# Kernel generation of a state-space mixer on one core: the lower half of the phase table stored with its four channels backwards, and its samples written out in two parts

## The chip, the cores and the metric

The program runs on one core of one Trainium2 chip. The metric is the device time of one execution in microseconds (us); lower is better. The engines are named as the profile names them: PE (matrix products; PEld is its weight load), DVE (elementwise work), ACT (activation functions and copies), POOL, and SP, which here only issues DMAs. "The profile" is one execution recorded by the hardware; its times count from the first instruction of the program.

## What is computed

One block of a sequence model: a state-space mixer and a channel MLP, each with a residual, on 2048 positions of 512 channels. Cut to what matters:

```python
dt = exp(log_dt)[:, None]                     # one step size per channel d
logdA = dt * (A_re + 1j * A_im)               # 512 channels x 128 states
P = exp(logdA[:, :, None] * l)                # powers at the positions l
K = einsum("dn,dnl,dn->dl", C, P, dt * B).real   # the convolution kernel, one per channel
y = irfft(rfft(u padded) * rfft(K padded))    # causal convolution along the positions
h = x + y + u * Dskip                         # u: layernorm of layernorm-ed x
out = h + gelu(layernorm(layernorm(h)) @ w1 + b1) @ w2 + b2
```

The change touches the second and third line from the top: how samples of K are made.

## The kernel before

The channels are done in two halves of 256 (`hh` = 0 and 1). A half is 64 groups `e` of four channels `g`. The kernel K is not made at all 2048 positions but at sample positions, as a product of two exponentials: a coarse one in 32 steps `k` of 8 positions, and a fine one at 20 offsets `m`.

- **`exps` (lines 659 to 688).** ACT fills the magnitudes: `K.Pt[128 states, 2, 64 e, 32 k, 4 g]`, its second plane `[:, 1]`, by 32 exponentials a half (line 673, one for each `k`, 256 columns, the four channels side by side), and `K.Q[128, 2, 64 e, 20 m, 4 g]` by 20 more (line 681). DVE multiplies Q by an amplitude (line 685).
- **`p_half` (lines 691 to 719).** A half has 8 blocks `b` of 8 groups `e`. For each, PE writes phases into PSUM (`pv`, line 703), ACT takes cosines and sines of them (line 142, tile `s`, two planes of 512 columns: 8 `e` x 16 `i` x 4 `g`), and DVE multiplies them into the magnitudes (`mul`, lines 709 to 714, all through the helper on line 79). The 16 phases serve 32 exponents: the upper ones, `k` = 16 + `i`, take `s` as it is, in one operation of 1024 columns for both planes; the lower ones, `k` = 15 - `i`, take the two planes of `s` exchanged, and run downwards in `k`. [...]
- **`q_half` (lines 722 to 751).** The same for Q: phases `qv`, sines `sq`, one product of 1024 columns on DVE for each of ten pieces a half.
- **`kgen` (lines 754 to 801).** For each group of four channels PE multiplies the Pt block (128 states x 128 columns `4k + g`) with the Q block (128 states x 80 columns) into `kps`. ACT or DVE moves eight groups at a time to the tile `samples`, called `all` in the code, `[128 rows 4k + g, 4 g, 20, 64 e]`: eight such moves a half. Of the four `g` of a row only that row's own is wanted: `put` (line 784) writes, for each `g`, the rows `g::4` to DRAM (`KD`), four transfers a half. `get` (line 794) then loads five arrangements of it back as `kt`, the operand of the next products.
- **`conv` (lines 895 to 1000).** PE makes the kernel's spectrum from `kt` and a table `M` (`kfps`, line 930), DVE multiplies it with the spectrum `X` of the input (`pa`, `pb`, `X`), PE turns it back (`zps`), ACT copies it (`z`), and it goes through DRAM (`Zd`, line 997) to `ZT` (line 995). The input's spectrum is made in `x_stage` (`xps`, lines 882 to 885) from `X`, which is loaded from `A_dram` in four transfers of 1 MB (line 865).

All instructions of this part are recorded as operations with engines that a list of numbers, `ORDER`, puts into one fixed order; each engine works through its own in that order, and so does the DMA queue of SP. Four things stand near the transfers of the samples. On SP, in the first half: two `put`, two transposing transfers (`R<-M`, line 479), a `get`, the fourth load of X, two small loads of `M` (line 462), a `get`; POOL has the other two `put` and three `get`. In the second half SP has all four `put`, then a `ZT` load, a `get`, two stores of `z`, and four `get`.

The MLP follows (lines 1194 to 1312).

Of the kernel before, what the change touches and what calls it, by code (L numbers as in the profile page):

```python
# [10 lines left out]
ACT = mybir.ActivationFunctionType  # L11
ALU = mybir.AluOpType
# [4 lines left out]
P = 128  # L17
# [60 lines left out]
def tt(nc, out, a, b, op, e="DVE"):  # L78
    (nc.vector if e == "DVE" else nc.gpsimd).tensor_tensor(out, a, b, op)  # L79


def bc(ap, shape):
    return ap.to_broadcast(shape)
# [3 lines left out]
def evac(nc, eng, out, in_):  # L87
    if eng in (0, "ACT"):
        nc.scalar.copy(out, in_)  # L89
    else:  # L90
        nc.vector.tensor_copy(out, in_)  # L91
# [35 lines left out]
def logs(nc):  # L127
    if NOW[0] != "logs":
        nc.scalar.preload_act_table_set("natural_log_exp_and_others")
    NOW[0] = "logs"  # L130
# [8 lines left out]
def sines(nc, out, v):  # L139
    NOW[0] = "sines"  # L140
    n = v.shape[-1]
    nc.scalar.activation(out, v.bitcast(i16)[..., 0:2 * n:2], ACT.Sin, scale=S2PI / 65536)  # L142
# [516 lines left out]
def exps(nc, S, K, big, hh, gate):  # L659
    ds = slice(HW * hh, HW * hh + HW)  # L660

    def get():
        K.Pt = big.tile([P, 2, HW // 4, 32, 4], bf16, name="Pt", tag="b1")
        K.Q = big.tile([P, 2, HW // 4, 20, 4], bf16, name="Q", tag="b2")

    K.o_get = S.op("NONE", 0.0, get, gate)
    K.o_pe, K.o_qe = [], []
    S.group = f"pe{hh}"
    for i in range(16):
        def amp(i=i):  # L670
            logs(nc)
            for k in (15 - i, 16 + i):
                nc.scalar.activation(K.Pt[:, 1, :, k, :], K.th[:, ds].rearrange("p (e g) -> p e g", g=4), ACT.Exp, scale=float(8 * k))  # L673

        K.o_pe.append(S.op("ACT", 0.62, amp, [K.o_th, K.o_get], fun=AT["exp"][hh]))
    S.group = f"qe{hh}"
    for n in range(5):
        def amp(n=n):
            logs(nc)
            for m in range(4 * n, 4 * n + 4):  # L680
                nc.scalar.activation(K.Q[:, 1, :, m, :], K.th[:, ds].rearrange("p (e g) -> p e g", g=4), ACT.Exp, scale=float(OFFS[m]))  # L681

        def mul(n=n):
            e = K.Q[:, 1, :, 4 * n:4 * n + 4, :]
            nc.vector.tensor_tensor(e, e, bc(K.amp[:, ds].rearrange("p (e g) -> p e g", g=4).unsqueeze(2), [P, HW // 4, 4, 4]), ALU.mult)

        x = S.op("ACT", 1.25, amp, [K.o_th, K.o_get], fun=AT["exp"][hh], bias=5.0)
        K.o_qe.append(S.op("DVE", 0.62, mul, [x, K.o_amp]))


def p_half(nc, S, K, sc, psp, hh):

    K.o_p = [[], []]
    for qd in range(2):
        S.group = f"p{hh}{qd}"
        for g in range(4):
            cell = {}
            b = 4 * qd + g

            def ph(cell=cell, b=b):  # L700
                v = cell["v"] = psp.tile([P, 2, 512], f32, name="pv", tag="p", bufs=PB)
                for u in range(2):
                    nc.tensor.matmul(v[:, u], lhsT=K.PQ[hh][:, b, :], rhs=K.RP[:, u].rearrange("p e i g -> p (e i g)"), start=True, stop=True)

            def sn(cell=cell):
                cell["s"] = sc.tile([P, 2, 8, 16, 4], bf16, name="s", tag="w", bufs=WB)
                sines(nc, cell["s"][:].rearrange("p u e i g -> p u (e i g)"), cell["v"][:])

            def mul(cell=cell, b=b):
                s, e = cell["s"], slice(8 * b, 8 * b + 8)  # L710
                hi = K.Pt[:, :, e, 16:32, :].rearrange("p u e k g -> p u e (k g)")
                tt(nc, hi, s[:].rearrange("p u e i g -> p u e (i g)"), bc(hi[:, 1:2], [P, 2, 8, 64]), ALU.mult)
                for u in range(2):
                    tt(nc, K.Pt[:, u, e, 15::-1, :], s[:, 1 - u], K.Pt[:, 1, e, 15::-1, :], ALU.mult)

            p = S.op("PE", 0.9, ph, [K.o_pl[hh], K.o_out[0], K.o_pe[8]], acq="p", bias=-10)
            K.o_phase[hh].append(p)
            x = S.op("ACT", 0.94, sn, [p] + K.o_pe + K.o_six, acq="w", rel=[p], fun=AT["sin"][hh])
            K.o_p[qd].append(S.op("DVE", 1.23, mul, [x] + K.o_pe, rel=[x]))
# [34 lines left out]
def kgen(nc, S, K, cv, sc, psp, hh, KD):  # L754
    cell = {}
    ends, mm = [], []
    for s in range(2):
        for b in range(4):
            e0 = 32 * s + 8 * b

            def mms(s=s, b=b, e0=e0):
                kps = cell[s, b] = psp.tile([P, 8, 128], f32, name="kps", tag="p", bufs=PB)
                for e in range(8):
                    for u in range(2):
                        nc.tensor.matmul(kps[:, e, 0:80], lhsT=K.Pt[:, u, e0 + e].rearrange("p k g -> p (k g)"),
                                         rhs=K.Q[:, u, e0 + e].rearrange("p m g -> p (m g)"), start=(u == 0), stop=(u == 1))

            def out(e, s=s, b=b, e0=e0):
                if not s and not b:
                    cell["all"] = sc.tile([P, 4, 20, 64], bf16, name="samples", tag="ko", bufs=1)  # L770
                evac(nc, e, cell["all"][:, :, :, e0:e0 + 8], cell[s, b][:, :, 0:80].rearrange("p e (m g) -> p g m e", g=4))

            first = not s and not b
            m = S.op("PE", 0.7, mms, [K.o_p[s][b], K.o_q[s][b], K.o_q[s][4]], acq="p")
            mm.append(m)
            ends.append(S.op(("ACT", "DVE"), (0.75, 0.75), out, [m] + (K.o_raw if first else ends[:1]), rel=[m], acq="ko" if first else None))
    K.o_kgen = mm
    ds = slice(HW * hh, HW * hh + HW)

    def q(e):  # L780
        return nc.sync if e == "SP" else nc.gpsimd

    def put(e, g):
        q(e).dma_start(KD[hh][32 * g:32 * g + 32].rearrange("p (r c) -> p r c", r=4)[:, :, 0:320], cell["all"][g::4, g].rearrange("p (r s) j -> p r (s j)", s=5))

    def get(e, t):
        if t == 0:
            K.kt[hh] = cv.tile([P, 5, HW], bf16, name="kt", tag="kt", bufs=2)
        if t < 2:
            src = KD[hh][:].rearrange("(g k) (r c) -> (k r) g c", g=4, r=8)[128 * t:128 * t + 128, :, 0:64]  # L790
        else:
            at = (64, 128, 256)[t - 2]
            src = KD[hh][:].rearrange("(g k) (r c) -> (k r) g c", g=4, r=4)[:, :, at:at + 64]
        q(e).dma_start(K.kt[hh][:, t, :].rearrange("p (g c) -> p g c", g=4), src)

    either = ("SP", "POOL")
    w = [S.op(either, (0.46, 0.8), lambda e, g=g: put(e, g), ends, rel=[ends[0]], lat=2.5) for g in range(4)]
    K.o_put = w
    K.o_kt[hh] = []
    for t in range(5):  # L800
        K.o_kt[hh].append(S.op(either, (0.46, 0.8), lambda e, t=t: get(e, t), w + K.o_kt[hh][:1], lat=2.5, acq="kt" if t == 0 else None))
# [651 lines left out]
```

## Time and profile before

| | |
|---|---|
| runs of the kernel before | 263.83, 269.31 and 265.45 us, median 265.45 |
| the profiled execution | 264.65 us |
| its span, first to last instruction | 262.9 us; 1.75 us lie around it |
| granted TensorE clock, mean | 0.991 |
| busy: PE, DVE, ACT | 222.3, 201.4, 178.5 us |

The sums below are made against the profiled execution, 264.65 us, which lies 0.8 us under the median of the three runs. In the rows of the profile, L79 and L91 are lines of helpers, so work is told apart by the names of its tiles: `Pt<-s,Pt` is the product of this change, `KD<-samples` its transfer. A row of the timeline reads: start, duration of the row, engine, line, operation, tiles, shape, count, and in brackets how long the engine had been idle and what ended that. Rows of equal instructions that follow each other are merged.

### The profile page before, as it was taken

How to read it: one execution, taken by the hardware profiler on the slowest of the kernel's cores; microseconds unless marked ns; L12 is line 12 of the kernel's file. 1: busy time of each engine (PE TensorE's matmuls, PEld its weight loads, DVE VectorE, ACT ScalarE, POOL GpSimd, SP SyncE). 2: the span in 40 equal slices, each digit the busy share in tenths (PEclk: the TensorE clock that was granted, in tenths of full speed). 3: DMA queues.
4: the chain of work that ended last, by engine and by line, in shares of the span. 5: the costliest groups of instructions: out<-in, count | busy, mean ns of one | idle time of the engine just before them, and what ended most of it. 6: DMA issues, size and time to landing. Idle time of an engine off the chain costs nothing.

```text
span 262.9 us, 4459 instructions
## 1 busy us (share of the span) xinstructions
PE 222.3 (85%) x1574; PEld 139.1 (53%) x1587; DVE 201.4 (77%) x445; ACT 178.5 (68%) x303; POOL 35.3 (13%) x96
## 2 busy tenths in 40 slices
PE   3999118856698598689999999879999999999994
PEld 2333002322496386468988888668844444444443
DVE  5999999999999969999789989757745764771022
ACT  4999999999999959998643666546704603622810
POOL 8806920000016000000520000000000000000000
PEclk9999999999999989999999999999999999999999
DMA  5804933588787700061197576979532033023001
GB/s 160 299 1 83 175 108 122 106 259 257 232 285 138 170 0 2 0 172 30 52 209 205 145 218 188 251 218 329 134 80 80 1 60 102 0 45 88 31 22 57
DMA packets 50450, 33.61 MB, mean 128 GB/s; under 512 B 22186, under 2 KB 49068, under 8 KB 50172
## 3 DMA queue, kind: packets, MB, share of 16 engines
q1 hardware_dynamic: 49068, 29.82, 41.8%
q0 software_dynamic: 1360, 3.51, 5.6%
q8 instruction: 12, 0.20, 0.3%
q14 instruction: 10, 0.08, 0.1%
HBM read 18.65 MB, written 11.26 MB: 114 GB/s over the span
## 4 chain that ended last, share of the span: by engine, by line
PE 44%; ACT 25%; DVE 13%; DMA 11%; issue 4%; SPq 2%; ACTq 0%; DVEq 0%
PE h1ps L1260 14%; PE o2ps L1273 13%; PE kfps L930 5%; ACT Pt L673 4%; DMA Zd<-z 4%; ACT a L89 4%; ACT sq L142 3%; DMA X<-A_dram 3%; ACT s L142 3%; ACT Q L681 2%; DVE pa L79 2%; DVE X L79 2%; DVE pb L79 2%; ACT z L89 2%; DVE Pt L79 1%
## 5 line engine op out<-in xcount | busy, mean ns | idle before, releaser
L1263 ACT ACTIVATE hT<-h1ps,b_sb 128x512 bf16<-128x512 f32 (+3 forms) x55 | 31.9, 604 | 41.0 <-PE h1ps L1260 39.2
L1260 PE MATMUL h1ps<-y2T,wide 128*128 128x512 bf16 (+3 forms) x217 | 40.2, 336 | 0.7 <-DVE ve L75 0.6
L930 PE MATMUL kfps<-kt,M 128*128 128x256 bf16 x320 | 38.7, 276 | 0.0
L1273 PE MATMUL o2ps<-w_sb,hT 128*128 128x512 bf16 (+3 forms) x183 | 38.5, 366 | 0.2
L79 DVE TENSOR_TENSOR ot<-o2ps,h 128x512 bf16<-128x512 f32 (+1 forms) x17 | 10.9, 658 | 30.6 <-PE o2ps L1273 21.2
L930 PEld LDWEIGHTS <-M 128*128 128x128 bf16 x320 | 31.8, 99 | 4.5 <-issue 0.2
L1260 PEld LDWEIGHTS <-wide 128*128 128x128 bf16 (+1 forms) x220 | 21.8, 100 | 17.0 <-issue 0.8
L1273 PEld LDWEIGHTS <-hT 128*128 128x128 bf16 (+1 forms) x187 | 18.3, 98 | 19.7
L79 DVE TENSOR_TENSOR Pt<-s,Pt 128x512 bf16<-128x512 bf16 (+1 forms) x48 | 22.8, 510 | 0.7 <-ACT s L142 0.2
L844 PE MATMUL aps<-u,BD 128*128 128x512 bf16 x30 | 10.1, 422 | 14.5 <-DVE u L839 11.0
L673 ACT ACTIVATE Pt<-th 128x256 bf16<-128x256 f32 x64 | 21.1, 405 | 0.9 <-DVE th L79 0.9
L142 ACT ACTIVATE sq<-qv 128x1024 bf16<-128x1024 int16 x20 | 20.9, 1079 | 0.0
L89 ACT CAST z<-zps 128x1024 bf16<-128x1024 f32 (+1 forms) x16 | 15.5, 976 | 2.8 <-PE zps L969 2.4
L142 ACT ACTIVATE s<-pv 128x1024 bf16<-128x1024 int16 x16 | 16.6, 1080 | 0.0
L89 ACT CAST a<-aps 128x1024 bf16<-128x1024 f32 x16 | 15.7, 1040 | 0.1
L738 PE MATMUL qv<-RQ,PQ 128*128 128x512 bf16 (+1 forms) x64 | 11.8, 298 | 4.2 <-ACT s L142 1.8
L844 PEld LDWEIGHTS <-BD 128*128 128x128 bf16 x32 | 2.9, 101 | 21.0 <-DVE u L839 15.4
L91 DVE CAST X<-xps 128x1024 bf16<-128x1024 f32 x11 | 12.9, 1217 | 1.3 <-PE xps L885 1.3
L449 POOL DMA_DIRECT2D Dp<-Dd x24 | 12.2, 517 | 9.8 <-DMA Dd<-ds 9.8
L79 DVE TENSOR_TENSOR Q<-sq,Q 128x1024 bf16<-128x1024 bf16 x20 | 13.1, 685 | 0.2
L681 ACT ACTIVATE Q<-th 128x256 bf16<-128x256 f32 x40 | 13.0, 403 | 0.0
L89 ACT CAST kf<-kfps 128x512 bf16<-128x512 f32 (+1 forms) x9 | 5.7, 633 | 10.7 <-PE kfps L930 7.0
(242 smaller groups left out, 441.0 us busy)
## 6 DMA issues: line engine op xcount, KB each, us to landing
A_dram<-a SPq DMA_DIRECT2D x16, 256.0 KB, 2.6
X<-A_dram SPq DMA_DIRECT2D x4, 1024.0 KB
Zd<-z SPq DMA_DIRECT2D x15, 256.0 KB, 3.8
ZT<-Zd SPq DMA_DIRECT2D x10, 256.0 KB, 4.0
x<-in_A_u_dram SPq DMA_DIRECT2D x4, 512.0 KB
X<-in_A_u_dram SPq DMA_DIRECT2D x4, 512.0 KB
out_dram<-ot SPq DMA_DIRECT2D x15, 128.0 KB, 1.7
ZT<-Zd POOLq DMA_DIRECT2D x6, 256.0 KB, 4.6
```

The lines of the kernel that those rows point to most:

```text
L79: (nc.vector if e == "DVE" else nc.gpsimd).tensor_tensor(out, a, b, op)
L89: nc.scalar.copy(out, in_)
L91: nc.vector.tensor_copy(out, in_)
L142: nc.scalar.activation(out, v.bitcast(i16)[..., 0:2 * n:2], ACT.Sin, scale=S2PI / 65536)
L449: nc.gpsimd.dma_start(t[o::128 // cnt], bass.AP(row.tensor, row.offset + 1024 * kh, [[0, cnt], [1, 1024]]))
L673: nc.scalar.activation(K.Pt[:, 1, :, k, :], K.th[:, ds].rearrange("p (e g) -> p e g", g=4), ACT.Exp, scale=float(8 * k))
L681: nc.scalar.activation(K.Q[:, 1, :, m, :], K.th[:, ds].rearrange("p (e g) -> p e g", g=4), ACT.Exp, scale=float(OFFS[m]))
L844: nc.tensor.matmul(ps[:, h, :], lhsT=K.BD[:, h].rearrange("p a b -> p (a b)"), rhs=cell["u"][:], start=True, stop=True)
L930: nc.tensor.matmul(ps[:, k, c, :], lhsT=K.M[:, t, k0 + k, c, :], rhs=kt[:, t, :], start=((plain or c == 1) and t == 0), stop=(t == 4))
L1260: nc.tensor.matmul(pt[:fs, 0:n], lhsT=K.w1_sb[:, dc, fc * P:fc * P + fs], rhs=(y2T[tb][:, dc, js, :] if tb or js.start else K.y2T[:, dc]). ...
L1263: nc.scalar.activation(hT[tb % 2][:fs, fc, cols], pt[:fs, 0:n], ACT.Gelu_apprx_tanh, bias=K.b1_sb[:fs, fc:fc + 1], scale=1.0)
L1273: nc.tensor.matmul(pt[:], lhsT=h[:fs, fc, jj * P:(jj + 1) * P], rhs=K.w2_sb[:fs, fc, d], start=(fc == 0), stop=(fc == NFC - 1))
```

## The change

The diff:

```diff
@@ exps @@
             for k in (15 - i, 16 + i):
-                nc.scalar.activation(K.Pt[:, 1, :, k, :], K.th[:, ds].rearrange("p (e g) -> p e g", g=4), ACT.Exp, scale=float(8 * k))
+                nc.scalar.activation(K.Pt[:, 1, :, k, :] if k > 15 else K.Pt[:, 1, :, k, ::-1], K.th[:, ds].rearrange("p (e g) -> p e g", g=4), ACT.Exp, scale=float(8 * k))
@@ p_half @@
                 s, e = cell["s"], slice(8 * b, 8 * b + 8)
                 hi = K.Pt[:, :, e, 16:32, :].rearrange("p u e k g -> p u e (k g)")
                 tt(nc, hi, s[:].rearrange("p u e i g -> p u e (i g)"), bc(hi[:, 1:2], [P, 2, 8, 64]), ALU.mult)
-                for u in range(2):
-                    tt(nc, K.Pt[:, u, e, 15::-1, :], s[:, 1 - u], K.Pt[:, 1, e, 15::-1, :], ALU.mult)
+                lo = K.Pt[:, :, e, 0:16, :].rearrange("p u e k g -> p u e (k g)")[:, :, :, ::-1]
+                tt(nc, lo, s[:, ::-1].rearrange("p u e i g -> p u e (i g)"), bc(lo[:, 1:2], [P, 2, 8, 64]), ALU.mult)
@@ kgen @@
     def put(e, g):
-        q(e).dma_start(KD[hh][32 * g:32 * g + 32].rearrange("p (r c) -> p r c", r=4)[:, :, 0:320], cell["all"][g::4, g].rearrange("p (r s) j -> p r (s j)", s=5))
+        for rows, at in ((slice(32 * g, 32 * g + 16), slice(3 - g, 64, 4)), (slice(32 * g + 16, 32 * g + 32), slice(64 + g, P, 4))):
+            q(e).dma_start(KD[hh][rows].rearrange("p (r c) -> p r c", r=4)[:, :, 0:320], cell["all"][at, g].rearrange("p (r s) j -> p r (s j)", s=5))
```

What it does. The magnitudes of the lower exponents, `k` < 16, are stored with their four channels backwards. Then (`k`, `g`) of the lower half, read from its last column to its first, is `i` and `g` of the phases in rising order, and both planes of the lower half are one operation of 1024 columns: its output and its second input step by -1 element in the innermost dimension (64 columns), and the first input takes the planes of `s` in exchanged order. In the samples, the rows of `k` < 16 come out as `4k + 3 - g`, those of `k` >= 16 as `4k + g`; so `put` has two transfers for each `g`, of 16 rows each, where it had one of 32.

The list `ORDER` is the same, so nothing changes its place; operations get shorter or longer lists of instructions. Three places show it.

On DVE, the first three blocks of the first half (`Pt<-s,Pt` is the product with the sines, `u` the normalised input, `PQ` the phases' operand). Before:

```order
L91 COPY PQ_203<-lps 128x2048
L79 TENSOR_TENSOR Pt<-s,Pt 128x2x8x64
L79 TENSOR_TENSOR Pt<-s,Pt 128x8x16x4 x2
L839 TENSOR_SCALAR u<-x,mv,rs_230 128x512
L79 TENSOR_TENSOR Pt<-s,Pt 128x2x8x64
L79 TENSOR_TENSOR Pt<-s,Pt 128x8x16x4 x2
L79 TENSOR_TENSOR Pt<-s,Pt 128x2x8x64
L79 TENSOR_TENSOR Pt<-s,Pt 128x8x16x4 x2
```

And now (a row of x2 is one block, a row of x4 two):

```order
L91 COPY PQ_203<-lps 128x2048
L79 TENSOR_TENSOR Pt<-s,Pt 128x2x8x64 x2
L840 TENSOR_SCALAR u<-x,mv,rs_230 128x512
L79 TENSOR_TENSOR Pt<-s,Pt 128x2x8x64 x4
L840 TENSOR_SCALAR u<-x,mv,rs_230 128x512
```

Three instructions of a block became two of the same shape; there are 16 blocks in the program.

On SP, from the first half's `put` to its last `get` (`KD` is the samples in DRAM, `kt` what is loaded from it, `R` a transposed table, `X` the input). Before:

```order
L865 DMA X<-A_dram 128x8x512 x3
L784 DMA KD_65<-samples 128x1x320 x2
L479 DMA_TRANSPOSE R<-M 128x4x128 x2
L794 DMA kt<-KD_65 128x4x64
L865 DMA X<-A_dram 128x8x512
L462 DMA M<-Bd 1x64x128 x2
```

And now:

```order
L866 DMA X<-A_dram 128x8x512 x3
L785 DMA KD_65<-samples 64x1x320 x4
L479 DMA_TRANSPOSE R<-M 128x4x128 x2
L795 DMA kt<-KD_65 128x4x64
L866 DMA X<-A_dram 128x8x512
L462 DMA M<-Bd 1x64x128 x2
```

Two more transfers stand ahead of the transposing ones, a `get` and the fourth load of X. POOL likewise has four `KD<-samples` where it had two, ahead of its three `get`.

On SP in the second half, where `KD_66` is that half's samples. Before:

```order
L784 DMA KD_66<-samples 128x1x320 x4
L995 DMA ZT<-Zd_67 16x8192
L794 DMA kt<-KD_66 128x4x64
L997 DMA Zd_67<-z 128x4x256 x2
L794 DMA kt<-KD_66 128x4x64 x4
```

And now:

```order
L785 DMA KD_66<-samples 64x1x320 x8
L996 DMA ZT<-Zd_67 16x8192
L795 DMA kt<-KD_66 128x4x64
L998 DMA Zd_67<-z 128x4x256 x2
L795 DMA kt<-KD_66 128x4x64 x4
```

Four more transfers stand ahead of all five `get` of that half.

## The prediction

> **What bounds the kernel now.** First the page: busy shares, the tenths in 40 slices of 6.57 us, and the shares of the chain that ended last.
>
> ```profile
> span 262.9 us, 4459 instructions
> PE 222.3 (85%) x1574; PEld 139.1 (53%) x1587; DVE 201.4 (77%) x445; ACT 178.5 (68%) x303; POOL 35.3 (13%) x96
> DVE  5999999999999969999789989757745764771022
> ACT  4999999999999959998643666546704603622810
> PE 44%; ACT 25%; DVE 13%; DMA 11%; issue 4%; SPq 2%; ACTq 0%; DVEq 0%
> ```
>
> The changed work lies between 49 and 126 us, slices 8 to 20. There DVE and ACT are both full, so a mean share decides nothing. The windows of the two stretches with the products, of the stretch in which ACT sets the pace, and of the one after:
>
> ```profile
> 49.00:77.60 28.60, 20.38 (x203) 11.66 (x206) 27.80 (x59) 28.48 (x34) 0.00 (x0) 1.00 0.85 251
> 97.10:126.00 28.90, 25.44 (x271) 18.87 (x272) 27.90 (x55) 26.69 (x30) 0.00 (x0) 1.00 0.17 46
> 98.40:120.70 22.30, 18.84 (x173) 13.39 (x175) 21.67 (x44) 22.27 (x24) 0.00 (x0) 1.00 0.22 60
> 128.00:145.00 17.00, 16.78 (x154) 14.70 (x152) 14.99 (x27) 7.36 (x10) 3.67 (x4) 1.00 0.76 180
> ```
>
> (Length, then busy PE, PEld, DVE, ACT, POOL.) In the first half DVE idles 0.8 us of 28.6 and ACT 0.1; in the second ACT idles 0.03 us of 22.3 and DVE 0.6; after 128 PE idles 0.2 of 17. So DVE work that grows is paid in full at once, while DVE work that shrinks uncovers ACT after the first fraction of a microsecond.
>
> How the first half ends, on DVE, then on ACT:
>
> ```profile
> 70.91 2.87 DVE L79 TENSOR_TENSOR Pt<-s,Pt 128x1024 bf16<-128x1024 bf16 x6
> 73.70 1.28 DVE L79 TENSOR_TENSOR Q<-sq,Q 128x1024 bf16<-128x1024 bf16 x2
> 74.90 0.69 DVE L73 TENSOR_SCALAR Mn<-M 128x2048 bf16<-128x2048 bf16 x1
> 75.50 1.29 DVE L79 TENSOR_TENSOR M<-base,Dp 128x1024 bf16<-128x1024 bf16 x2
> 76.71 0.82 DVE L91 CAST samples<-kps 128x640 bf16<-128x640 f32 x1
> ```
>
> ```profile
> 70.95 2.07 ACT L142 ACTIVATE sq<-qv 128x1024 bf16<-128x1024 int16 x2
> 72.77 3.81 ACT L89 CAST samples<-kps 128x640 bf16<-128x640 f32 x6
> ```
>
> The samples are complete at 76.71 + 0.82 = 77.53 by DVE, though ACT's part is done at 72.77 + 3.81 = 76.58. What follows on SP's queue, on POOL, and on PE:
>
> ```profile
> 77.60 1.17 SPq L784 DMA_DIRECT2D KD<-samples  x2
> 78.83 2.58 SPq L479 DMA_TRANSPOSE R<-M  x2
> 81.60 0.43 SPq L794 DMA_DIRECT2D kt<-KD  x1
> 82.49 1.17 SPq L865 DMA_DIRECT2D X<-A_dram  x1
> ```
>
> ```profile
> 78.10 1.33 POOL L784 DMA_DIRECT2D KD<-samples  x2 [43.87 <-issue]
> ...
> 81.59 2.27 POOL L794 DMA_DIRECT2D kt<-KD  x3 [2.16 <-DMA KD<-samples]
> ```
>
> ```profile
> 90.83 0.33 PE L882 MATMUL xps<-X,M 128*128 128x256 bf16 x1 [2.44 <-DMA X<-A_dram]
> ```
>
> PE waits 2.44 us for the fourth load of X, which stands on SP behind the samples' transfers. This queue, and not DVE or PE, carries the delay from 77.6 to 90.8.
>
> The second half, on SP, with the landing time of the last `get` and the PE row that needs it:
>
> ```profile
> 127.53 2.64 SPq L784 DMA_DIRECT2D KD<-samples  x4
> 130.28 0.57 SPq L995 DMA_DIRECT2D ZT<-Zd  x1
> 131.66 0.37 SPq L794 DMA_DIRECT2D kt<-KD  x1
> 132.49 0.91 SPq L997 DMA_DIRECT2D Zd<-z  x2
> 133.45 2.60 SPq L794 DMA_DIRECT2D kt<-KD  x4
> ...
> 137.37 2.33 SPq L1015 DMA_DIRECT2D wide<-Ds  x4
> ```
>
> ```profile
> L794 SPq DMA_DIRECT2D kt<-KD x2: 507/542/577, 134.9 to 135.5; - x2
> ...
> DMA to landing us min/median/max: 2.8/2.8/2.8
> ```
>
> ```profile
> 138.75 1.47 PE L930 MATMUL kfps<-kt,M 128*128 128x256 bf16 x12
> ```
>
> The last `get` starts at 135.5 and lands at 138.3; PE begins to use it at 138.75, without a gap. The margin is 0.45 us.
>
> **The change, part by part.** (1) *The product.* A block now: two operations of 512 columns and one of 1024. The row at 70.91 holds two blocks, and the next row starts at 73.70, so a block takes (73.70 - 70.91) / 2 = 1.40 us. An operation of 1024 columns takes (74.90 - 73.70) / 2 = 0.60 us from start to start. If the new one runs like the old upper one, a block takes 1.20 us: 0.20 us less, 1.6 us in each half. Its price is not in the trace: no DVE row here is known to step backwards in its innermost dimension. The nearest rows:
>
> ```profile
> L79 DVE TENSOR_TENSOR Pt<-s,Pt 128x512 bf16<-128x512 bf16 x32 | 13.5, 422 | 0.5
> L79 DVE TENSOR_TENSOR Pt<-s,Pt 128x1024 bf16<-128x1024 bf16 x16 | 11.0, 685 | 0.2 <-ACT s L142 0.2
> L91 DVE CAST X<-xps 128x1024 bf16<-128x1024 f32 x11 | 12.9, 1217 | 1.3 <-PE xps L885 1.3
> ```
>
> Between 512 and 1024 columns of bf16 lie 263 ns, 0.51 ns a column; the operation on f32 out of PSUM pays 1217 ns for 1024, about 1.04 ns a column after the same start. These are the ends, 685 and 1217 ns. I take 685: the row of 422 ns is the nearest, since it already writes and reads with `k` falling, in runs of four columns, at the fast rate (512 columns at the slow rate would be 422 + 0.53 x 512 = 693 ns).
>
> [...]
>
> What 1.6 us less on DVE gives in the first half: its last Q product waits for ACT's last `sq`, 70.95 + 2.07 = 73.02. From there Q 0.60, Mn 0.60 (75.50 - 74.90) and the two M 1.21 (76.71 - 75.50) put the move of samples at 75.43 and its end at 76.25. Then ACT's end at 76.58 is late next: SP starts at 76.66 instead of 77.60, 0.94 us earlier. In the second half I take 0: ACT is full from 98.4 to 120.7, PE from there on, so they cover what DVE saves.
>
> (2) *The exponentials.* Half of the Pt exponentials write each four columns backwards.
>
> ```profile
> L673 ACT ACTIVATE Pt<-th 128x256 bf16<-128x256 f32 x64 | 21.1, 405 | 0.9 <-DVE th L79 0.9
> ...
> L489 ACT ACTIVATE M<-M 128x256 bf16<-128x256 bf16 x2 | 1.3, 794 | 2.2 <-DMA M<-in_A_log_dt_dram 2.2
> ```
>
> I take 0: as before, they write runs of four with a jump between them, and another direction within a run is nearer to that than anything else. The far end is the scattered exponential of line 489, 794 ns: 32 x 0.39 = 12.4 us of ACT, hardly hidden in the first half. A gain would need fewer than 405 ns for 256 columns, for which nothing speaks.
>
> (3) *The transfers, first half.* Each half of a `put` costs SP an issue of its own. Two puts took 78.83 - 77.60 = 1.23 us. That half the rows make an issue cheaper is not what the queue shows: four `wide<-Ds` took 2.33 us, 0.58 each, and these are of 8 KB:
>
> ```profile
> wide<-Ds SPq DMA_DIRECT2D x8, 8.0 KB
> ...
> KD<-samples SPq DMA_DIRECT2D x6, 80.0 KB, 2.0
> ```
>
> So two more cost 1.23 us (ends: 0.0, if two halves issue like one whole, and 1.23). With the 0.94 us from (1), the transposes, the `get` and the load of X come 0.29 us later: X is issued at 82.78. POOL's two more, at 1.33 / 2 = 0.67 each, end at 78.10 - 0.94 + 2.67 = 79.83 and land some 2.1 us later, at 81.9, 0.3 us behind the 81.59 of before; the same shift. PE, waiting for X, passes it on. First half: +0.3 us.
>
> (4) *The transfers, second half.* Four more on SP: 130.28 - 127.53 = 2.75 us. Part falls into waits of SP: between 130.85 and 131.66 it waited for the last put to land, between 132.03 and 132.49 for `z`; 1.27 us, of which some 0.15 us stay as gaps between issues. The first `get` now needs only the first parts: the seventh put starts at 127.53 + 6 x 0.69 = 131.66 and lands, after the 2.0 us of the row above, at 133.7, just when SP comes to it. So the `get` are late by 2.75 - 1.12 = 1.6 us; the last lands at 139.9. PE wants it at 138.75, or 0.4 us later for the fifth product: it waits 0.8 to 1.2 us, I take 1.0. PE has no gap in the 17 us around (window above), and DVE and the stores of `z` wait for its `kfps`, so this goes to the end.
>
> Sum: 264.65 + 0.3 + 1.0 = 265.95, say **266.0 us**. Against the median of the runs, 265.45, it would be 0.5 more.
>
> **The rivals.** *A: the backward operation runs at the slow rate.* The product loses once the new operation takes more than 1.40 - 0.60 = 0.80 us from start to start, and the whole is over 2% slower from about 1.03 on (2% of 264.65 is 5.3 us; less the transfers' 2.2, with DVE's idle 0.6 added, it is 3.7 over 16 blocks, 0.23 on top of 0.80). At 1217 ns it takes from start to start what this row gives, (4.61 - 1.22) / 3 = 1.13 us:
>
> ```profile
> 79.23 4.61 DVE L91 CAST X<-xps 128x1024 bf16<-128x1024 f32 x4
> ```
>
> A block takes 0.60 + 1.13 = 1.73 us, 0.33 more, 2.7 us a half. DVE's idle time takes a little of it, as an estimate 0.4 of the 0.8 us idle in the first window and 0.2 of the 0.6 in the third; 2.3 and 2.5 us remain, and both halves end on DVE. The transfers' 1.23 and 1.0 are paid on top: 264.65 + 2.3 + 1.2 + 2.5 + 1.0 = 271.65, about 271.6 us. For it: no backward row in the trace. Against it: the 422 ns. This one ends slower by over 2%.
>
> *B: two half transfers issue like one.* Then the first half keeps its 0.94 us and the second loses nothing: 263.7 us. For it: the same number of bytes and rows in all. Against it: the 8 KB issues at 0.58 us.
>
> *C: the work on DVE gets shorter, but nothing in front of SP does* (ACT's moves end later than before, since PE makes `kps` in the same places). Then 264.65 + 1.2 + 1.0 = 266.9 us. It lies within the range of the forecast.
>
> **How the numbers follow.** The forecast with C, 264.3 to 267.5 us: 0.62. A, with rates between the two as well, 268 to 272.5: 0.28. B, 263 to 264.3: 0.07. Slow exponentials, or something else: 0.03. The range from 263.6 to 271.8 us leaves out the tails of A and B and the last case, some 2 in 10. The forecast's own range is 264.3 to 267.5. Faster by over 2%, about what a measurement of this kernel can tell from no change, would be under 260: no case gives it, 0.02. Slower by over 2%, over about 270, is most of A: 0.23. Within 2%: 0.75.
>
> **What would show it.** In the profile after: the row `Pt<-s,Pt 128x1024`, x32, at 685 ns on average (A: near 950, half of them at 1217); the first `KD<-samples` on SP near 76.7 (A: near 79.9); its four rows at 2.4 us together (B: 1.2); PE's wait for X still there; a new wait of PE for `kt` of about 1 us at the first `kfps` of the second half; and ACT's `Pt<-th` at 405 ns. I am wrong if the backward step costs a rate, or if SP's issues shrink with their rows.

## The result, and the profile after

The kernel after takes 267.22 us (median of 20 runs, 264.79 to 269.92), the kernel before, beside it on the same chip, 264.33 us (20 runs, 262.30 to 269.31). The ratio is 1.007, 95% interval 1.0043 to 1.0098: some 1.9 us slower, a small difference but a sure one. The ratio is taken over the executions within 1.5% of their kernel's fastest (16 of the 20 after, 17 of the 20 before); the medians are over all, and lie further apart, 2.9 us. The profiled execution of the kernel after took 265.38 us, with a span of 263.6.

First the price that no row had shown, the product that steps backwards, and the exponentials that write backwards. The page's groups, after:

```profile
L673 ACT ACTIVATE Pt<-th 128x256 bf16<-128x256 f32 x64 | 21.1, 405 | 0.9 <-DVE th L79 0.9
L79 DVE TENSOR_TENSOR Pt<-s,Pt 128x1024 bf16<-128x1024 bf16 x32 | 20.3, 688 | 0.4 <-ACT s L142 0.2
```

All 32 products of 1024 columns take 688 ns on average, where the 16 upward ones of before took 685: a step of -1 in the innermost dimension costs nothing that can be seen here. The exponentials stay at 405 ns. The line with the instruction counts has DVE at 429 instructions and 200.1 us busy (445 and 201.4 before).

This execution runs late by 0.9 us before the changed work begins. The copy ahead of the first product, in before and then in after:

```profile
47.88 1.22 DVE L91 COPY PQ<-lps 128x2048 bf16<-128x2048 bf16 x1
```

```profile
48.77 1.22 DVE L91 COPY PQ<-lps 128x2048 bf16<-128x2048 bf16 x1
```

Below, 0.89 us are taken off a time of after where it is compared with before. I read nothing from it: of the nine experiments with the changed product, five profiled executions have this copy at 47.9 us and four at 48.7. (The four profiled executions with the product of before all have it at 47.9, too few to tell whether the change has a part in it.)

The end of the first half, after: DVE, then SP's queue, then POOL.

```profile
70.34 0.69 DVE L79 TENSOR_TENSOR Q<-sq,Q 128x1024 bf16<-128x1024 bf16 x1 [0.25 <-ACT sq L142]
71.25 0.69 DVE L79 TENSOR_TENSOR Q<-sq,Q 128x1024 bf16<-128x1024 bf16 x1 [0.22 <-ACT sq L142]
71.86 2.49 DVE L79 TENSOR_TENSOR Pt<-s,Pt 128x1024 bf16<-128x1024 bf16 x4
...
77.28 0.82 DVE L91 CAST samples<-kps 128x640 bf16<-128x640 f32 x1
```

```profile
78.17 2.50 SPq L785 DMA_DIRECT2D KD<-samples  x4
80.71 3.62 SPq L479 DMA_TRANSPOSE R<-M  x2
84.95 0.37 SPq L795 DMA_DIRECT2D kt<-KD  x1
85.38 0.49 SPq L866 DMA_DIRECT2D X<-A_dram  x1
```

```profile
78.67 2.37 POOL L785 DMA_DIRECT2D KD<-samples  x4 [43.53 <-issue]
82.83 2.27 POOL L795 DMA_DIRECT2D kt<-KD  x3 [1.79 <-DMA KD<-samples]
```

SP begins its four transfers at 78.17, less 0.89 is 77.28: 0.32 us earlier than the 77.60 of before, not 0.94. DVE now catches up with ACT's `sq` twice before its last blocks, and waits; from the start of that copy to the end of the last move of samples it is busy 27.85 us instead of 28.85, but idle 1.48 instead of 0.80. The four transfers take 2.50 us, as forecast; but the transposing ones behind them take 3.62 where they took 2.58, so the fourth load of X goes out at 85.38 - 0.89 = 84.49, 2.0 us later than the 82.49 of before.

The chain that ended last, from 78 to 95 us, runs through just this queue. Before, then after (start, duration, what):

```profile
78.83 1.27 SPq L479
...
80.14 1.26 SPq L479
...
82.49 8.30 DMA X<-A_dram
```

```profile
80.71 1.28 SPq L479
...
82.03 2.30 SPq L479
...
85.38 6.72 DMA X<-A_dram
```

Of the two transposing transfers only the second grew, from 1.26 to 2.30 us. In this execution the load itself took 6.72 us instead of 8.30, which gives back a good part of the delay; PE resumes here, waiting longer than before (2.44):

```profile
92.14 0.40 PE L883 MATMUL xps<-X,M 128*128 128x256 bf16 x1 [3.11 <-DMA X<-A_dram]
```

The second half, after: SP's queue, then PE at the first product that needs the last `get`.

```profile
128.60 5.48 SPq L785 DMA_DIRECT2D KD<-samples  x8
134.18 0.54 SPq L996 DMA_DIRECT2D ZT<-Zd  x1
134.89 0.45 SPq L795 DMA_DIRECT2D kt<-KD  x1
135.39 1.05 SPq L998 DMA_DIRECT2D Zd<-z  x2
136.54 2.84 SPq L795 DMA_DIRECT2D kt<-KD  x4
```

```profile
139.81 0.64 PE L931 MATMUL kfps<-kt,M 128*128 128x256 bf16 x2
141.07 4.31 PE L931 MATMUL kfps<-kt,M 128*128 128x256 bf16 x38 [0.62 <-DMA kt<-KD]
```

The new wait for `kt` is there, 0.6 us and a little at the product ahead of it. But 30 us later PE met another wait in before, for `ZT`, at its first `yh`, and that one is gone in after. Before, then after:

```profile
169.76 0.38 PE L1031 MATMUL yh<-ZT,Dm 96*128 96x256 bf16 x2 [0.91 <-DMA ZT<-Zd]
```

```profile
170.88 0.38 PE L1032 MATMUL yh<-ZT,Dm 96*128 96x256 bf16 x2
```

Whether the one wait took up the other, two executions can't tell. So this one execution, at 0.9 us late from the start, is 0.7 us longer at its end. It shows where things moved, not why the kernels differ by 1.9 us. That is for the experiments.

### The profile page after: what moved, and what is told of

Same layout as the page of the kernel before. It is cut to its first block, busy times and chain, and to the rows that moved or that the text cites. A ratio compares the mean times of both kernels' runs of the same rounds, so it can differ in the third digit from the quotient of the medians.

```text
span 263.6 us, 4476 instructions
## 1 busy us (share of the span) xinstructions
PE 223.8 (85%) x1587; PEld 138.9 (53%) x1587; DVE 200.1 (76%) x429; ACT 178.6 (68%) x303; POOL 35.9 (14%) x98
## 3 DMA queue, kind: packets, MB, share of 16 engines
HBM read 18.65 MB, written 11.26 MB: 113 GB/s over the span
## 4 chain that ended last, share of the span: by engine, by line
PE 48%; DVE 18%; ACT 18%; DMA 6%; SPq 5%; issue 4%; ACTq 0%; DVEq 0%
PE h1ps L1261 15%; PE o2ps L1274 14%; PE kfps L931 8%; ACT a L89 3%; DMA X<-A_dram 3%; ACT s L142 3%; ACT sq L142 3%; DVE Pt L79 2%; DVE X L79 2%; ACT Pt L673 2%; DVE five L79 2%; DVE pa L79 2%; DVE pb L79 2%; DVE Q L79 1%; ACT Q L681 1%
## 5 line engine op out<-in xcount | busy, mean ns | idle before, releaser
L79 DVE TENSOR_TENSOR Pt<-s,Pt 128x1024 bf16<-128x1024 bf16 x32 | 20.3, 688 | 0.4 <-ACT s L142 0.2
```

## The experiments

Theory 1: the sample transfers that were added to the queues cost the time. Theory 2: the product and the exponentials do. Ratios are against the kernel before, run on the same chip; a profiled execution is a single one, and two of the same kernel may differ by more than 1 us (the 20 of before lie between 262.30 and 269.31).

**The product alone.** The changed product and storage, but whole sample transfers as before:

```diff
     def put(e, g):
-        for rows, at in (...):
-            q(e).dma_start(KD[hh][rows]..., cell["all"][at, g]...)
+        q(e).dma_start(KD[hh][32 * g:32 * g + 32]..., cell["all"][g::4, g]...)
```

> The product with the backward step alone: the lower half's channels are stored backwards, but each of the eight transfers of samples is whole again, 32 rows as before, so that the rows of the lower exponents go out with their channels in exchanged places (the output is therefore another one; the work and its shapes are those of the change). Theory 1 (the added transfers on the queues cost the time): the kernel is no slower than before, about 0.3 us faster, since the profile after shows the samples' first transfer 0.3 us earlier when counted from the copy of the phases: ratio 0.997 to 1.001, about 264 us. Theory 2 (the product, or the exponentials that write backwards, cost the time): ratio about 1.007 as with the whole change, 266.2 us.

Measured: 0.9992 (0.9946 to 1.0037). Product and exponentials neither cost nor gain anything that can be seen.

**The split alone.** Product and storage of before; each sample transfer in two parts:

```diff
     def put(e, g):
-        q(e).dma_start(KD[hh][32 * g:32 * g + 32]..., cell["all"][g::4, g]...)
+        for rows, at in ((slice(32 * g, 32 * g + 16), slice(g, 64, 4)), (slice(32 * g + 16, 32 * g + 32), slice(64 + g, P, 4))):
+            q(e).dma_start(KD[hh][rows]..., cell["all"][at, g]...)
```

> The transfers alone: the product and the storage as before, each transfer of samples in two of 16 rows, so eight in the first half (four on SP, four on POOL) and eight on SP in the second. Theory 1: slower by what both halves pay without DVE's gain, 1.2 + 1.0 us less some of it that later waits take up: ratio 1.005 to 1.009, about 266 us; PE's wait for kt at the first kfps of the second half is about 1 us. Theory 2: ratio 0.998 to 1.002, 264.3 us.

Measured: 1.0075 (1.0038 to 1.0113), the whole of the loss. Theory 1 holds, theory 2 falls.

**Which half.** The changed kernel with whole transfers in the second half, then in the first: in `put`, `if hh == 1:` (or `if hh == 0:`) the single transfer of 32 rows.

> The whole change, but the second half's transfers are whole again, 32 rows each (the lower rows of that half go out with channels exchanged, so the output is another one). Theory 1: only the first half's delay is left, two more issues on SP less 0.3 us of DVE's gain: ratio 1.001 to 1.005, about 265.0 us, and PE does not wait for kt at the second half's first kfps. Theory 2: ratio 1.007, 266.2 us.

> The whole change, but the first half's transfers are whole again, 32 rows each (the lower rows of that half go out with channels exchanged, so the output is another one). Theory 1: the second half's wait for kt is left, 1.0 us, less DVE's 0.3 us in the first half: ratio 1.001 to 1.005, about 265.0 us; the fourth load of X is issued as early as before. Theory 2: ratio 1.007, 266.2 us. A third theory, that only one of the halves matters: one of this kernel and the one with the second half whole is at 1.007 and the other at 1.000.

Measured: whole in the second half 1.0058 (1.0008 to 1.0108), whole in the first 1.0001 (0.9959 to 1.0044). Neither expectation of 1.001 to 1.005 for both was met; the points lie as the third theory has them, and the loss goes with the first half's transfers. The two intervals overlap a little, so this rests on the next experiment too. The second half's split alone costs nothing that can be told from zero, though 1.0 us, 0.4%, is still inside that interval. Its wait is there, as the kernel whole in the first half shows on PE, at `kfps` and at `yh`:

```profile
137.03 3.22 PE L934 MATMUL kfps<-kt,M 128*128 128x256 bf16 x28 [0.53 <-DMA kt<-KD]
```

```profile
167.15 0.38 PE L1035 MATMUL yh<-ZT,Dm 96*128 96x256 bf16 x2 [0.25 <-DMA ZT<-Zd]
```

It waits 0.53 us for `kt`, and 0.25 for `ZT` where before waited 0.91.

**The load of X ahead.** If the first half's transfers cost time by holding up the load of X, then moving that load ahead of them must undo the loss. One number in `ORDER`, first in the changed kernel, then in the kernel before:

```diff
-    ... 1313, 1253, 1256, ... 1264, 1480, 1296, 1464, ...
+    ... 1313, 1296, 1253, 1256, ... 1264, 1480, 1464, ...
```

> The changed kernel, with one step moved in the order: the fourth load of X is issued on SP right ahead of the first half's sample transfers instead of behind two transposing transfers and a get. The output is the reference's. Queue theory (the first half's extra transfers cost time because they hold up SP, and with it the fourth load of X, for which PE waits 3.1 us): PE's wait for X falls below 1 us, the first kfps comes at about 91.5 us instead of 94.0, and the time is no longer above the kernel before: ratio 0.985 to 1.000. Rival, landing theory (the cost is in the transfers themselves, that land later and so make kt late): the wait moves to kt, the first kfps stays at 93.5 or later, and the ratio stays at 1.005 or above.

> The kernel before, with the same one step moved: the fourth load of X ahead of the first half's sample transfers. Queue theory: the 2.4 us that PE waits for X in the kernel before are also paid to SP's queue; most go, the ratio is 0.985 to 0.997, and the changed kernel with the same move is level with it within 0.4%. Landing theory: the 1 MB of X then lies ahead of the samples on the DMA engines, the gets land later, and the ratio is 1.00 or above.

Measured: the load goes out at 70 us, and the ratios are 0.997 (0.9928 to 1.0011) and 0.9955 (0.9919 to 0.999); the medians are 262.60 and 262.63 us, beside 264.65 for the kernel before. No loss of the changed kernel can be seen any more, and the kernel before gains too. By their means, the changed kernel with the move is 0.4 us slower than the kernel before with it, give or take 1.0, where the change had cost 1.9. PE in the changed kernel with the load ahead:

```profile
91.12 0.27 PE L929 MATMUL kfps<-top,ones 128*128 128x256 bf16 x1 [1.06 <-ACT X L89]
91.23 1.25 PE L931 MATMUL kfps<-kt,M 128*128 128x256 bf16 x10
```

The wait for X is gone; the next late thing is ACT's move of a finished `xps`. The landing theory had the wait go to `kt`. POOL's `get` did come later, at 86.23 instead of 82.83, with X ahead of the samples on the DMA engines, but that was still in time.

**Which queue.** The changed kernel with whole transfers in the first half, on SP only, then on POOL only (`if hh == 0 and e == "SP":`, or `"POOL"`).

> The changed kernel, but in the first half the two sample transfers that SP issues are whole ones of 32 rows, as before; POOL's two stay in two parts each, and so does the second half. The lower rows of SP's two then hold exchanged channels, so this is not the reference's result. If SP's two extra issues are what costs: the fourth load of X is issued 1 us or more earlier than in the changed kernel (85.4 us) and the ratio is 1.000 to 1.003. If POOL's extra issues cost (they hold up its gets, and the issues on SP that overlap them take longer): the ratio stays at 1.005 to 1.008, and one of SP's issues between 80 and 88 us still takes 0.7 to 1 us longer than its like.

> The changed kernel, but in the first half the two sample transfers that POOL issues are whole ones of 32 rows; SP's two stay in two parts each, and so does the second half. The lower rows of POOL's two then hold exchanged channels, so this is not the reference's result. If SP's two extra issues are what costs: ratio 1.005 to 1.008. If POOL's are: 1.000 to 1.003, and the second transposing transfer is issued in about 1.3 us again, not 2.3. If either alone is enough to make X late, or if each costs half, both this run and its counterpart lie between, 1.002 to 1.005.

Measured: SP's whole 1.0051 (1.0005 to 1.0097), POOL's whole 1.0021 (0.9979 to 1.0064). Neither one alone restores 1.000 for sure, and the two intervals overlap, so the share of each queue is not settled. Both points lie where POOL's extra issues were to put them. One of that theory's signs came, with POOL's whole: the two transposing transfers take 2.58 us again, not 3.62. The other did not: with SP's whole no issue behind is 0.7 us longer (the load of X, 0.83 beside 0.49, is the nearest). "SP's extra issues alone" is not supported: with SP's whole the load of X does go out 2.35 us earlier (83.03, not 85.38), yet the ratio stays above 1, and the profile has a second path, over POOL. Its later `get` make PE wait for `kt` right behind X:

```profile
90.92 0.28 PE L886 MATMUL xps<-X,M 128*128 128x256 bf16 x1 [2.17 <-DMA X<-A_dram]
93.21 0.93 PE L934 MATMUL kfps<-kt,M 128*128 128x256 bf16 x7 [0.81 <-DMA kt<-KD]
```

**X later, with no transfer added.** The kernel before, with that load moved behind the second `get`:

```diff
-    ... 1264, 1480, 1296, 1464, ... 1372, 1276, 1512, ...
+    ... 1264, 1480, 1464, ... 1372, 1276, 1296, 1512, ...
```

> The kernel before, with one step moved in the order: the fourth load of X is issued on SP behind the two small loads of M and the second get, at about 85.6 us instead of 82.5; the sample transfers stay whole and the product as it was. The output is the reference's. Queue theory (the time follows the issue of this load, whatever holds it up): PE's wait for X grows from 2.4 us to 4 to 5.5 us and the ratio is 1.006 to 1.015, at least the changed kernel's 1.007, without a single transfer more. Rival (the split transfers cost time by themselves, by their number or landing): the ratio stays within 0.997 to 1.003.

Measured: 1.0123 (1.0082 to 1.0163). The load went out at 86.97, later than the 85.6 expected, and PE waited 3.95 us, just under the expected 4 to 5.5:

```profile
92.74 0.28 PE L882 MATMUL xps<-X,M 128*128 128x256 bf16 x1 [3.95 <-DMA X<-A_dram]
```

So the delay of this load alone, without one split transfer, costs as much as the change and more. The issue does not fix the landing, though: the load took 5.73 us here and 8.30 in before, so that PE went on only 1.9 us later for an issue 4.5 us later. The rest of the 3.2 us is not traced; the granted clock, by its median over the executions, was 0.980 here and 0.993 in the kernel before beside it.

**Is DVE's saving worth anything once PE no longer waits for X?** The product alone (first experiment) with the load of X ahead.

> The changed kernel with whole sample transfers in both halves (the lower rows then hold exchanged channels, so this is not the reference's result) and with the fourth load of X ahead of the first half's sample transfers: the shorter product alone, with PE no longer waiting for X. If DVE's saving of 1.6 us a half was worth something and only hidden behind the wait for X, this is faster than the kernel before with the same move (ratio 0.9955): 0.987 to 0.992. If other work covers it (ACT's casts and sines, and PE), it is level with that one: 0.993 to 0.998.

Measured: 0.9954 (0.9924 to 0.9983), beside 0.9955 of the kernel before with the same move. Nothing that can be seen: other work covers what DVE saves.

**How much delay the second half can take.** The changed kernel with X ahead, and four parts for each transfer of the second half:

```diff
+        if hh == 1:
+            for n in range(4):
+                at = slice(32 * n + (3 - g if n < 2 else g), 32 * n + 32, 4)
+                q(e).dma_start(KD[hh][32 * g + 8 * n:32 * g + 8 * n + 8]..., cell["all"][at, g]...)
+            return
```

> The changed kernel with the fourth load of X ahead, and in the second half each sample transfer in four parts of 8 rows instead of two of 16: sixteen issues on SP instead of eight. The output is the reference's. The eight more, at 0.6 us, make the gets of that half 4 to 5 us later; PE's wait for kt grows from about 0.5 us to 4 to 5.5 us. Slack theory (a wait of up to about 1 us is given back where PE later waits for ZT, a longer one is not): the first yh comes 3 to 4.5 us later and the ratio is 1.008 to 1.015. Rival (the end does not hang on the second half's kt at all): the waits for ZT vanish or PE catches up elsewhere, and the ratio stays at 0.996 to 1.000.

Measured: 1.0251 (1.0217 to 1.0284), more than any theory had. SP's sixteen issues, then PE:

```profile
124.75 11.26 SPq L787 DMA_DIRECT2D KD<-samples  x16
```

```profile
139.86 0.27 PE L936 MATMUL kfps<-kt,M 128*128 128x256 bf16 x1 [3.73 <-DMA kt<-KD]
142.24 0.37 PE L936 MATMUL kfps<-kt,M 128*128 128x256 bf16 x1 [2.12 <-DMA kt<-KD]
143.07 6.14 PE L936 MATMUL kfps<-kt,M 128*128 128x256 bf16 x38 [0.46 <-DMA kt<-KD]
```

The waits sum to 6.3 us, above the 4 to 5.5 expected: an issue took 0.70 us, not 0.6. What was missed is the last row: the 38 products that took 4.31 us in the kernel after take 6.14. PE's granted clock was 0.79 in the stretch with the waits, and 0.68 in the 6 us behind it. The windows of this kernel from 135.8 and from 143 us (length, busy PE, PEld, DVE, ACT, POOL, then the granted clock):

```profile
135.80:143.00 7.20, 0.97 (x6) 0.35 (x4) 3.25 (x5) 1.01 (x1) 1.11 (x3) 0.79 0.70 161
143.00:149.00 6.00, 5.93 (x38) 4.52 (x38) 1.23 (x2) 0.59 (x1) 0.36 (x1) 0.68 1.05 303
```

So a delay of this size goes to the end, with a lowered clock on top, and the rival falls. The slack theory named the direction, but not the size, and its slack is not shown to be the wait for `ZT`. PE still waits for `ZT` here, and it does so in the kernel with SP's transfers whole, which waits 0.62 us for `kt` as well. This kernel's first `yh` on `ZT`, then that one's:

```profile
175.58 0.38 PE L1037 MATMUL yh<-ZT,Dm 96*128 96x256 bf16 x2 [0.79 <-DMA ZT<-Zd]
```

```profile
169.82 0.38 PE L1035 MATMUL yh<-ZT,Dm 96*128 96x256 bf16 x2 [0.82 <-DMA ZT<-Zd]
```

The kernel before with X ahead, on the other hand, has no wait for `kt` and only 0.17 us for `ZT`. What can be said is the sum. From the second half's first `put` on SP to this `yh` row, the six profiled executions with whole transfers in that half take 41.48 to 42.32 us, the seven with two parts 41.87 to 42.93. The means, 41.85 and 42.23, are 0.4 us apart; with four parts it is 50.83.

**The clock behind the wait for X.** The same stands behind the wait for X in the first half. Windows of the kernel after, during PE's wait, in the 3 us behind it, and in the next 3:

```profile
88.90:92.00 3.10, 0.13 (x2) 0.00 (x0) 3.10 (x5) 3.10 (x10) 0.00 (x0) 0.96 0.86 203
92.00:95.00 3.00, 2.86 (x14) 2.07 (x15) 0.94 (x2) 3.00 (x11) 0.19 (x1) 0.50 0.04 2
95.00:98.00 3.00, 3.00 (x29) 2.63 (x28) 1.82 (x3) 1.70 (x6) 0.00 (x0) 0.98 0.00 0
```

The lowered stretch is some 3.4 us long: 3.0 in the middle window, 0.25 and 0.12 by the 0.96 and 0.98 of its neighbours. Is this part of the loss? The last kernel fills the wait with products:

```diff
             ps = cell["p"] = psp.tile([P, 2, 2, HW], f32, name="xps", tag="p", bufs=PB)
+            if hh == 0 and k == 14:
+                for _ in range(24):
+                    nc.tensor.matmul(ps[:, 0, 0, :], lhsT=K.Mn[:, 0, :], rhs=K.Mn[:, 0:2, :], start=True, stop=True)
```

> The changed kernel, unchanged in its transfers and its order; ahead of the products that wait for the fourth load of X, PE does 24 extra products of 256 columns from a table into the same PSUM tile, some 2.6 us, which the next product overwrites. The output is the reference's. In the changed kernel PE is idle there for 3.1 us, then its granted clock is 0.50 for 3.6 us and a product takes 421 ns instead of 273. Clock theory (the wait for X costs twice: the wait itself, and slower products after it because PE was idle): the granted clock stays at 1.00, the first ACT copy of F comes 1 to 1.5 us earlier than in the changed kernel (99.5), and the ratio falls from 1.007 to 1.000 to 1.004. Rival (the lower clock costs nothing, since other engines set the pace there, or does not come from the idle time): the ratio stays at 1.005 to 1.010.

Measured: 1.0068 (1.0024 to 1.0112), no better than the change itself. PE and, below, the windows of the same three stretches:

```profile
89.32 2.78 PE L882 MATMUL xps<-Mn 128*128 128x256 bf16 x24
93.59 0.27 PE L886 MATMUL xps<-X,M 128*128 128x256 bf16 x1 [1.49 <-DMA X<-A_dram]
```

```profile
88.90:92.00 3.10, 3.00 (x27) 2.48 (x26) 3.10 (x5) 3.10 (x10) 0.00 (x0) 1.00 0.91 208
92.00:95.00 3.00, 1.51 (x14) 1.26 (x13) 0.54 (x2) 3.00 (x11) 0.19 (x1) 1.00 0.09 4
95.00:98.00 3.00, 3.00 (x30) 2.69 (x28) 2.42 (x3) 1.89 (x7) 0.00 (x0) 1.00 0.00 0
```

The clock stayed at 1.00, as it should if the idle time is what lowers it (one execution, and no proof: the last section has one whose clock stayed up with nothing filled in). But in this execution X came 1.45 us later than in the kernel after (93.59 and 92.14), which ate what the clock gave. The ratio shows no gain, so this run claims no share of the 0.7% for the clock.

The executions on record say more. Their mean granted clock comes in steps of some 0.0065, which is what one stretch of 3.4 us at 0.50 takes off 263 us. The kernel before, from the four sets that ran beside the experiments, and the kernel after (seven executions of before between 0.914 and 0.940 are left out):

| mean granted clock | before: executions, mean us | after: executions, mean us |
|---|---|---|
| 0.998 to 1.000 | 19, 262.8 | none |
| 0.991 to 0.994 | 34, 264.1 | 8, 265.3 |
| 0.984 to 0.987 | 33, 265.2 | 6, 267.3 |
| 0.978 to 0.981 | 5, 266.9 | 6, 268.6 |
| 0.972 to 0.973 | 6, 268.2 | none |

A step goes with 1.1 to 1.7 us in the kernel before, and that is most of the spread between its executions. At the same clock the kernel after is 1.1 to 2.1 us slower, so the loss is not the clock alone. But it lies 1.9 steps below the top row on average, the kernel before 1.4; at 1.3 us a step that would be some 0.6 us, an estimate, and a weak one, since the sets ran on other chips.

## Why the prediction was right, and where its steps were not

The forecast, 1.3 us above the profiled execution of before, and no difference beyond 2%, came out: the ratio gives 1.9 us, and the median of 267.22 lies in the forecast's own range of 264.3 to 267.5. Its two main terms, though, were in the wrong places.

1. *The product* (685 ns taken, ends 685 and 1217): 688 measured. This was the choice on which rival A's 0.28 hung, and the row that decided it, runs of four columns with `k` falling at 422 ns for 512, was the right one: beside the 685 of before, the step of -1 shows no price.
2. *The exponentials* at 0: 405 ns, as taken.
3. *The transfers, first half* (+0.3 us): the term that failed. Its two parts were 1.23 us for two more issues and 0.94 us of gain from DVE. The issues came as said (2.50 us for four). The gain did not: SP started 0.32 us earlier instead of 0.94. I had followed DVE's queue from ACT's last `sq` only, and that queue has Q products ahead of the last Pt blocks, which wait for earlier `sq`: 0.25 and 0.22 us of new idle time, of 0.68 in all. And the second transposing transfer took 1.0 us more, which nothing in the trace of before announced. That belongs to the split: in the four kernels with all the first half's transfers in two parts and X behind them it took 2.01 to 2.30 us, in the six with some or all of them whole 1.26 to 1.29. Why is open. Together the load of X is issued 2.0 us later, not 0.3; the runs put the price of the first half's split at about 0.7% (1.007 with it, 1.0001 without).
4. *The transfers, second half* (+1.0 us, "so this goes to the end"): the wait came near its size, 0.6 us in one row and 0.7 in all, but little of it went to the end: 0.4 us are left at the first `yh` on `ZT`, and 0.4, give or take 1.0, in the times of the two kernels with X ahead. I had checked 17 us for gaps of PE and concluded from them for the rest of the program. Where the delay goes is open: the wait for `ZT` at 169.8 in before looked like the place, but the other runs do not bear it out. That there is a limit, the run with four parts shows.

That the two errors nearly cancel (0.6 to 1.0 us too much in the second half, some 1.2 to 1.5 too little in the first) is luck. Rival A fell with the 688 ns. B fell with the 2.50 us for four half transfers. C, 266.9 us, with DVE's gain not passed on, came nearest in the time: the gain is worth nothing that shows in the runs (0.9992, and 0.9954 beside 0.9955). But C's second term was as wrong as mine, and its reason is not what the trace shows: the last move of samples before SP starts is still DVE's, which ends at 78.10, and not ACT's, at 77.53.

## What to carry to other kernels

A transfer of samples cost its queue 0.6 to 0.7 us at each of the three sizes that ran (2.64 us for four of 80 KB, 2.50 for four of 40, 11.26 for sixteen of 20), so count what stands *behind* the added ones on that queue, and above all a large load that an engine will wait for; moving that one load ahead made both kernels faster (262.6 us) than they were without it. To say that a delay goes to the end, follow the work to the end, not over the next stretch. Compare executions of the same granted clock before a microsecond is explained. A saving on an engine is worth something only where its next instructions do not wait for another engine (DVE's was worth nothing that shows, 0.9954 beside 0.9955): look at each wait in its queue, not only at the last.

## What the runs showed of the hardware

- Around the end of a wait PE's granted clock was in several executions 0.50 for some 3.4 us (the three windows under "The clock behind the wait for X"; where PE waited again, in the kernel with four parts, its two windows give 3.0 and 3.8). By windows of 0.5 us the lowered stretch begins 0.4 us ahead of the end of the wait in after (3.11 us), 0.1 us behind it in before (2.44 us), and 1.2 us behind it in the kernel before with X later (3.95 us); it is 3.4 us long in all three. The length of the idle time alone does not decide. In before it was 0.50 after 2.44 us of waiting for X; in the kernel with POOL's transfers whole it was 1.00 after the same 2.44 us. The windows of the 3 us from 91 to 94, before and then that kernel:

```profile
91.00:94.00 3.00, 3.00 (x16) 2.14 (x15) 1.68 (x3) 3.00 (x11) 0.19 (x1) 0.50 0.01 1
```

```profile
91.00:94.00 3.00, 3.00 (x30) 2.67 (x28) 2.03 (x3) 3.00 (x11) 0.19 (x1) 1.00 0.00 0
```

  PE completes 16 products in the one and 30 in the other. So two waits of the same length can end differently; what decides, no run here shows. Single executions of one kernel differ by such stretches, at 1.1 to 1.7 us each in the kernel before.
- One of SP's issues sometimes takes 0.7 to 1.1 us longer than its like (in before the load of X 1.17, in after 0.49; with the product alone SP's first `get` 1.55, in before 0.43). Which one it is differs from kernel to kernel, and some have none (with POOL's two whole the load of X takes 0.51, the two `get` 0.37 and 0.46). In the four kernels with all the first half's transfers in two parts and X behind, it is each time the second transposing transfer (2.30, 2.01, 2.15 and 2.10 us). With POOL's two whole it is back at 1.26, with SP's two whole at 1.29, so neither queue's extra transfers alone make it long. How they do it was not tried.
